# Top-32 attention with a gated feed-forward: batch 0 takes its score products in plain fp32 on 64 partitions

## The chip, the core and the metric

The kernel runs on one core of one Trainium2 chip. The metric is device time in microseconds (us) of one execution. The kernel before takes 1626.93 us, the median of 3 runs (1625.65 to 1627.8).

## What is computed

The inputs are q, k and v of 8 batches, 8 heads, 576 positions and 64 head dimensions, and three weights of a gated feed-forward network. Cut to what matters:

```
scores = 1/sqrt(64) * q @ k.T                   # (8, 8, 576, 576)
kth    = the 32nd largest score of each row
scores = where(scores >= kth, scores, -1e9)
attn   = exp(scores - rowmax) / sum             # softmax over the kept ones
x      = (attn @ v), heads side by side         # (4608, 512)
out    = (sigmoid(x @ w_gate) * (x @ w_val)) @ w_out
```

The second part has 1536 hidden units, and 4608 tokens in all.

## The kernel before

Three dimensions cut the attention. A batch has four head pairs (p), and each head has five query tiles (i): four of 128 rows, and a last one in which the remaining 64 rows of both heads of a pair stand side by side. One step of the program is one (pair, query tile): 20 steps to a batch, 16 with two heads one after the other (J = 2) and 4 with the shared tile (J = 1). The steps of a batch run in two groups; in batch 0 the first group holds query tiles 0 to 2 of all four pairs (12 steps), the second tiles 3 and 4 (8 steps).

A step goes through these stages:

- `load_keys`, `load_queries` (L154, L172) bring transposed keys and queries into memory. The host has written each of them twice, on partitions 0 to 63 and again on 64 to 127. The keys of a head (128x576) are rounded by ScalarE (ACT) to the short format fp32r (L161), and on partitions 64 to 127 GpSimd (POOL) puts the rest, raw minus rounded, in their place, in two halves (L163). A query tile (128x256) is rounded on ACT (L176) to `qh`, and POOL makes `ql`, raw minus rounded (L177). A product over 128 partitions with `qh` and one with `ql` then add up to the product of the unsplit numbers, to the precision of the parts.
- `scores` (L180) makes these two fp32r products for each half of 288 keys (L195), and ACT copies a head's row of 576 from PSUM (L202). The PSUM tile has one buffer.
- `select` (L243) is mostly VectorE (DVE): maxima of 8 segments (L260), three rounds of maxima and replacement over the 64 candidates (L264, L266); then ACT's sign (L272), POOL's product with it (L278), a last maximum on DVE (L286), ACT's exponential (L209) and DVE's masked product (L214).
- `turn` and `weigh` (L289, L308): TensorE (PE) transposes the probabilities (L297, L302), multiplies them by the values in plain fp32 (L316 to L324), and the result is stored as a rounded part and a rest, `xh` and `xl`.
- `ffn` works on units of 384 tokens with fp32r weights and three products for each (L372 to L374, L391 to L393).

Before use, each of 18 weight blocks is split into two fp32r parts as well (`split_weight`, L116): two halves to a block, each with three DVE instructions (L136 to L138), three PE products (L144 to L146), and work of ACT and POOL (L135, L139, L141, L143, L147). Twelve blocks are split during the first group of batch 0, one to a step; the last six when the first unit of the feed-forward comes to them.

What orders the work: the main loop (L437) issues scores two steps ahead (`AHEAD`), queries four (`ASK`) and the keys and values of the next pair (`fetch`); the feed-forward is let in by the number of tokens done (L462), with a lag of `BEHIND` = 480 tokens. A scheduler then lays the recorded instructions out on each engine by its own model of their times; each engine takes its list in order.

Of the kernel before, what the change touches and what calls it, by code (L numbers as in the profile page):

```python
# [28 lines left out]
def tile_topk_attention_then_gated_ffn(  # L29
# [32 lines left out]
    BEHIND = 480  # L62

    LOADED, HELD = 12, 0

    const = ctx.enter_context(tc.tile_pool(name="const", bufs=1))
    bi = ctx.enter_context(tc.tile_pool(name="bi", bufs=4))
# [86 lines left out]
    def load_keys(b, p, nm):  # L154

        ks = []
        for h in (2 * p, 2 * p + 1):
            raw = bkr.tile([P, S], F32, tag="kraw", name=f"kraw_{nm}_{h}")
            nc.sync.dma_start(raw, k[b, h])
            kt = bk.tile([P, S], F32R, tag="k", name=f"k_{nm}_{h}")  # L160
            nc.scalar.activation(kt, raw, AF.Copy)  # L161
            for c in (slice(0, HALF), slice(HALF, S)):
                nc.gpsimd.tensor_tensor(kt[D:, c], raw[D:, c], kt[D:, c], op=ALU.subtract)  # L163
            ks.append(kt)
        return ks
# [4 lines left out]
        return vt  # L170

    def load_queries(b, i, p):  # L172
        raw = bqr.tile([P, 2 * P], F32, tag="qraw", name=f"qraw_{b}_{i}_{p}")
        nc.sync.dma_start(raw, q[b, i, p])
        qh, ql = [bq.tile([P, 2 * P], F32R, tag=t, name=f"{t}_{b}_{i}_{p}") for t in ("qh", "ql")]
        nc.scalar.activation(qh, raw, AF.Copy)  # L176
        nc.gpsimd.tensor_tensor(ql, raw, qh, op=ALU.subtract)  # L177
        return qh, ql

    def scores(qs, ks, i, nm):  # L180

        J = 2 if i < NT else 1
        s = bs.tile([P, 2, S], F32, tag="s", name=f"s_{nm}")
        for j in range(J):
            ps = ps_s.tile([P, 2, 512], F32, tag="s", name=f"pss_{nm}_{j}")
            for half in range(2):

                parts = [(j, 0, HALF, half * HALF)]
                if i == NT:

                    m = S - REM - HALF
                    parts += [(1, 0, HALF, REM)] if half == 0 else [(1, 0, m, REM + HALF), (1, m, REM, 0)]
                todo = [(x, part) for part in parts for x in qs]
                for t, (x, (h, o, n, k0)) in enumerate(todo):
                    nc.tensor.matmul(  # L195
                        ps[:, half, o : o + n],
                        x[:, h * P : (h + 1) * P],
                        ks[h][:, k0 : k0 + n],
                        start=t == 0,
                        stop=t == len(todo) - 1,  # L200
                    )
# [371 lines left out]
```

## Time and profile before

| | |
|---|---|
| median of 3 runs | 1626.93 us |
| the profiled execution's own time | 1628.2 us |
| its span, first to last instruction | 1626.3 us |
| mean granted TensorE clock | 0.977 |
| PE busy | 1546.3 us (95%), 10226 instructions |
| PE weight loads busy | 1399.8 us (86%) |
| DVE busy | 1285.6 us (79%) |
| POOL busy | 1238.9 us (76%) |
| ACT busy | 1174.1 us (72%) |

The shares are means over a start, a long middle and an end, which differ; the stretches are read apart in the rows further down. A granted clock of 1.00 is TensorE's upper level, 2.4 GHz, and 0.50 the lower, 1.2 GHz; a mean in between says how long each level was held. Matmul ends are modelled, so what a matmul costs in a row of them is read from the distance between starts. A plain fp32 matmul leaves two records in the trace, an fp32r matmul one.

### The profile page before, as it was taken

The numbers are of one execution on the slowest core, as the hardware profiler recorded it, in microseconds if no ns is written. First come the engines' busy times: TensorE is split into PE (matmuls) and PEld (weight loads), VectorE is DVE, ScalarE is ACT, GpSimd is POOL, SyncE is SP. The second block draws the span as 40 slices with busy tenths as digits, with TensorE's granted clock in tenths as the row PEclk, the third lists the DMA queues.
The fourth block names the chain that finished last, engine by engine and source line by source line (L and its number), as shares of the span: only waits on it lengthen the run. The fifth ranks groups of instructions, "written<-read, shape, count | busy, mean of one in ns | idle before, by whom it ended". The sixth has DMA issues, their size and how long they took to land.

```text
span 1626.3 us, 33530 instructions
## 1 busy us (share of the span) xinstructions
PE 1546.3 (95%) x10226; PEld 1399.8 (86%) x10226; DVE 1285.6 (79%) x5748; ACT 1174.1 (72%) x2643; POOL 1238.9 (76%) x1959
## 2 busy tenths in 40 slices
PE   5777899899999999999999999999999999999998
PEld 3444797689999999989999999999899999999997
DVE  6999868988988778878888778889888778878310
ACT  8898668877777777677777777778677777767321
POOL 8889868898876887787776896788876987776413
PEclk8887999999999999999999999999999999999999
DMA  7546754566565665566564665565555665554574
GB/s 259 186 161 201 266 203 167 186 225 217 189 218 178 219 236 198 184 207 227 193 206 178 219 239 195 196 230 195 203 199 178 216 224 198 184 198 164 195 265 178
DMA packets 89182, 332.58 MB, mean 204 GB/s; under 512 B 9888, under 2 KB 36512, under 8 KB 62112
## 3 DMA queue, kind: packets, MB, share of 16 engines
q1 hardware_dynamic: 88992, 330.34, 58.7%
q8 instruction: 83, 1.36, 0.3%
q14 instruction: 107, 0.88, 0.2%
HBM read 301.99 MB, written 28.31 MB: 203 GB/s over the span
## 4 chain that ended last, share of the span: by engine, by line
PE 75%; DVE 5%; POOL 5%; ACT 4%; issue 1%; POOLq 0%; ACTq 0%; DVEq 0%
PE pz L372 11%; PE pz L374 11%; PE pz L373 11%; PE pss L195 8%; PE po L316 6%; PE pt L297 6%; PE po L391 6%; PE po L392 5%; PE po L393 5%; PE po L318 2%; POOL u L278 2%; DVE e L214 2%; ACT e L209 1%; PE po L327 1%; DVE kths L286 1%
## 5 line engine op out<-in xcount | busy, mean ns | idle before, releaser
L278 POOL TENSOR_TENSOR u<-s,under 128x288 f32<-128x288 f32 x576 | 446.1, 796 | 89.0 <-ACT under L272 82.7
L260 DVE MAX8 cand<-s 128x8 f32<-128x72 f32 x2304 | 346.7, 217 | 81.4 <-ACT s L202 80.7
L372 PE MATMUL pz<-xh,w 128*128 128x384 f32 x1120 | 383.3, 344 | 1.7 <-ACT part L398 1.7
L373 PE MATMUL pz<-xl,w 128*128 128x384 f32 x1120 | 379.5, 339 | 0.0
L374 PE MATMUL pz<-xh,w 128*128 128x384 f32 x1120 | 379.4, 339 | 0.0
L214 DVE SCALAR_TENSOR_TENSOR e<-s,kths,e 128x576 f32<-128x576 f32 x288 | 297.1, 1035 | 1.9 <-ACT e L209 1.8
L286 DVE MAX8 kths<-u 128x8 f32<-128x584 f32 x288 | 219.7, 763 | 71.0 <-POOL u L279 69.0
L272 ACT ACTIVATE under<-s,leads 128x576 bf16<-128x576 f32 x288 | 223.2, 776 | 42.2 <-DVE leads L264 38.0
L209 ACT ACTIVATE e<-s,st 128x576 f32<-128x576 f32 x288 | 210.7, 773 | 57.5 <-POOL st L268 57.4
L380 POOL TENSOR_TENSOR gl<-gf,gh 128x384 fp32r<-128x384 f32 x144 | 153.5, 1066 | 88.8 <-ACT gh L379 86.3
L202 ACT ACTIVATE s<-pss 128x576 f32<-128x576 f32 x288 | 185.3, 643 | 39.0 <-PE pss L195 38.9
L372 PEld LDWEIGHTS pz<-xh,w 128*128 128x128 f32 x1120 | 210.9, 188 | 2.5 <-ACT part L398 2.0
L195 PE MATMUL pss<-k,qh 128*128 128x288 f32 (+2 forms) x672 | 200.6, 316 | 13.1 <-ACT qh L176 6.6
L373 PEld LDWEIGHTS pz<-xl,w 128*128 128x128 f32 x1120 | 210.9, 188 | 0.4 <-issue 0.3
L374 PEld LDWEIGHTS pz<-xh,w 128*128 128x128 f32 x1120 | 210.7, 188 | 0.0
L298 ACT ACTIVATE et<-pt 128x384 f32<-128x384 f32 x384 | 180.8, 489 | 36.5 <-PE pt L297 35.6
L297 PE MATMUL pt<-ident,e 128*128 128x128 f32 x1152 | 188.0, 280 | 16.6 <-DVE e L214 14.9
L392 PE MATMUL po<-gl,w 128*128 128x384 f32 x560 | 192.2, 344 | 0.4 <-POOL gl L380 0.4
L391 PE MATMUL po<-gh,w 128*128 128x384 f32 x560 | 189.4, 352 | 1.8 <-ACT part L398 0.9
L393 PE MATMUL po<-gh,w 128*128 128x384 f32 x560 | 189.7, 340 | 0.0
L195 PE MATMUL pss<-k,ql 128*128 128x288 f32 (+2 forms) x672 | 185.1, 298 | 1.0 <-POOL ql L177 1.0
L297 PEld LDWEIGHTS pt<-ident,e 128*128 128x128 f32 x1152 | 145.4, 144 | 37.9 <-DVE e L214 16.2
(100 smaller groups left out, 3339.2 us busy)
## 6 DMA issues: line engine op xcount, KB each, us to landing
w<-ws SPq DMA_DIRECT2D x210, 1024.0 KB, 5.0
v<-in_v_dram SPq DMA_DIRECT2D x64, 352.0 KB, 3.4
qraw<-in_q_dram SPq DMA_DIRECT2D x160, 128.0 KB, 2.8
kraw<-in_k_dram SPq DMA_DIRECT2D x64, 288.0 KB, 3.4
wraw<-in_w_dram SPq DMA_DIRECT2D x36, 512.0 KB, 4.1
ws<-wsplit SPq DMA_DIRECT2D x36, 512.0 KB, 4.0
out_dram<-acc SPq DMA_DIRECT2D x48, 192.0 KB, 3.6
```

Of the source, the lines that this page charges most:

```text
L195: nc.tensor.matmul(ps[:, half, o : o + n], x[:, h * P : (h + 1) * P], ks[h][:, k0 : k0 + n], start=t == 0, stop=t == len(todo) - 1,)
L214: nc.vector.scalar_tensor_tensor(e[:, j], s[:, j], kth[j], e[:, j], op0=ALU.is_ge, op1=ALU.mult, accum_out=st[:, 4 + j : 5 + j])
L260: nc.vector.max(cand[:, j, 8 * g : 8 * g + 8], s[:, j, g * SEG : (g + 1) * SEG])
L278: nc.gpsimd.tensor_tensor(u[:, j, c], s[:, j, c], under[:, j, c], op=ALU.mult)
L286: nc.vector.max(kths[:, at[j] : at[j] + 8], u[:, j])
L297: nc.tensor.transpose(pt[:, c], ef[:, k0 : k0 + P], ident)
L372: nc.tensor.matmul(ps, wt[:, u, 0, d], xh, start=d == 0, stop=False)
L373: nc.tensor.matmul(ps, wt[:, u, 0, d], xl, start=False, stop=False)
L374: nc.tensor.matmul(ps, wt[:, u, 1, d], xh, start=False, stop=d == NP - 1)
L391: nc.tensor.matmul(ps, wt[:, e % 2, 0, f], gh, start=f == 0, stop=False)
L392: nc.tensor.matmul(ps, wt[:, e % 2, 0, f], gl, start=False, stop=False)
L393: nc.tensor.matmul(ps, wt[:, e % 2, 1, f], gh, start=False, stop=f == FG - 1)
```

## The change

Batch 0 no longer splits keys and queries. Its keys and queries are loaded as fp32, the first 64 partitions only, and one plain fp32 product over 64 partitions stands in place of the two fp32r products over 128. The other seven batches are as before.

```diff
+    WHOLE = 1
...
     def load_keys(b, p, nm):
         ks = []
         for h in (2 * p, 2 * p + 1):
+            if b < WHOLE:
+                kt = bk.tile([P, S], F32, tag="k", name=f"k_{nm}_{h}")
+                nc.sync.dma_start(kt[:D], k[b, h][:D])
+                ks.append(kt)
+                continue
...
     def load_queries(b, i, p):
+        if b < WHOLE:
+            whole = bq.tile([P, 2 * P], F32, tag="qh", name=f"q_{b}_{i}_{p}")
+            nc.sync.dma_start(whole[:D], q[b, i, p][:D])
+            return (whole,)
...
     def scores(qs, ks, i, nm):
         J = 2 if i < NT else 1
+        K = D if len(qs) == 1 else P
...
                     nc.tensor.matmul(
                         ps[:, half, o : o + n],
-                        x[:, h * P : (h + 1) * P],
-                        ks[h][:, k0 : k0 + n],
+                        x[:K, h * P : (h + 1) * P],
+                        ks[h][:K, k0 : k0 + n],
```

In instructions: 8 roundings of keys and 20 of queries leave ACT; 16 key differences and 20 query differences leave POOL; 168 fp32r products leave PE and 84 plain fp32 ones come (64 of 288 columns, and four times 288, 288, 288, 224 and 64). The DMAs of batch 0's keys and queries keep their number, 8 and 20, at half the bytes.

The scheduler lays out all lists anew. Lines of the changed kernel stand 2 further down in `split_weight`, and 12 further down from `scores` on (L214 is then the eviction of the scores, L226 the masked product, L272 and L276 the maxima, L298 the last maximum, L384 the first feed-forward product).

ACT at the start of the program, before: five roundings (L161, L176) stand ahead of the first score eviction (`s`, L202).

```order
L161 ACTIVATE k_0_0_165<-kraw_0_0_163 128x576
L161 ACTIVATE k_0_1_171<-kraw_0_1_169 128x576
L176 ACTIVATE qh_0_0_179<-qraw_0_0_177 128x256
L176 ACTIVATE qh_1_0_185<-qraw_1_0_183 128x256
L176 ACTIVATE qh_2_0_191<-qraw_2_0_189 128x256
L135 ACTIVATE wt_lead_0_230<-wraw_0_228 128x512
L139 ACTIVATE wsplit_227<-wraw_0_228 128x512
L202 ACTIVATE s_0_0_201<-pss_0_0_0_202 128x576
```

The same place in the changed kernel:

```order
L214 ACTIVATE s_0_0_177<-pss_0_0_0_178 128x576
L137 ACTIVATE wt_lead_0_198<-wraw_0_196 128x512
L141 ACTIVATE wsplit_195<-wraw_0_196 128x512
L137 ACTIVATE wt_lead_1_215<-wraw_1_213 128x512
L141 ACTIVATE wsplit_195<-wraw_1_213 128x512
L214 ACTIVATE s_0_0_177<-pss_0_0_1_182 128x576
```

The first eviction of scores now stands ahead of the first weight block's work, and the five roundings are gone.

PE where the first feed-forward product comes (`pz`), before; `wrest` is the first product of the last half of the twelfth weight block, and `pss` are scores of the last head pair:

```order
L297 MATMUL pt_3_1_1_2387<-ident,e_3_1_2009 128x128 x2
L195 MATMUL pss_3_3_0_2285<-k_3_6_1154,qh_3_3_1988 128x288
L195 MATMUL pss_3_3_0_2285<-k_3_6_1154,ql_3_3_1989 128x288
L195 MATMUL pss_3_3_0_2285<-k_3_6_1154,qh_3_3_1988 128x288
L195 MATMUL pss_3_3_0_2285<-k_3_6_1154,ql_3_3_1989 128x288
L144 MATMUL wrest_1_1691<-wraw_1_1688,ident 128x512
L372 MATMUL pz_0_0_0_2146<-xh_0_684,w_0_2142 128x384
```

The same place in the changed kernel:

```order
L339 MATMUL po_3_0_1894<-ident,inv_3_0_1779 128x128
L317 MATMUL pt_4_0_1_2067<-ident,e_4_0_1751 64x128
L309 MATMUL pt_3_1_0_2191<-ident,e_3_1_1831 128x128 x3
L146 MATMUL wrest_1_1547<-wraw_1_1544,ident 128x512
L384 MATMUL pz_0_0_0_1959<-xh_0_612,w_0_1955 128x384
```

In both, the feed-forward stands right behind that `wrest`, which needs DVE's work on the block's last half (`wraw`). Ahead of it stand 154 of batch 0's 168 score products before, and 75 of 84 now; 123 transposes (L297) before and 120 now. On DVE, the list up to that `wraw` is 19 instructions shorter now: ten segment maxima, four candidate maxima, three replacements, one masked product and one product of `weigh` come later. Up to the `wraw` of the last of the 18 blocks it is 16 shorter.

## Rows read from the trace of the kernel before

**Rows 1.** Busy time of each engine in four stretches of the span (start, length, then busy us and number of instructions of each engine, the mean granted TensorE clock, the DMA share and rate).

```profile
0.00:180.00 180.00, 123.99 (x573) 79.05 (x573) 164.51 (x672) 156.90 (x327) 157.74 (x240) 0.83 0.62 208
180.00:260.00 80.00, 77.84 (x529) 72.54 (x527) 60.64 (x257) 50.25 (x115) 60.53 (x97) 1.00 0.59 209
260.00:330.00 70.00, 62.45 (x349) 48.33 (x347) 64.14 (x256) 62.17 (x133) 56.61 (x81) 0.95 0.59 195
330.00:1560.00 1230.00, 1223.33 (x8446) 1142.22 (x8447) 991.35 (x4556) 890.84 (x2042) 947.04 (x1526) 1.00 0.59 204
```

The columns of busy time are PE, PE's weight loads, DVE, ACT, POOL.

**Rows 2.** DVE's waits in the first 180 us (who waited for whom: us in total, times, the longest).

```profile
DVE wt_lead L136 <- ACT wt_lead L135: 9.6, 1, 9.6
DVE kths L286 <- POOL u L279: 2.8, 4, 1.4
```

**Rows 3.** The timeline, in order of time, around the places where the feed-forward begins (start, us, engine, line, operation, tiles, count, idle before and its releaser), and the line of the `wrest` products over the whole run (min, median and max in ns; first and last start).

```profile
179.29 1.17 PE L144 MATMUL wrest<-wraw,ident 128*128 128x512 f32 x2 [0.90 <-DVE wraw L137]
179.87 0.76 PE L372 MATMUL pz<-xh,w 128*128 128x384 f32 x1
...
L144 PE MATMUL wrest<-wraw,ident x72: 609/617/1224, 10.8 to 324.4; 128*128 128x512 f32 x72
```

**Rows 4.** The timeline of the first 12 us, some rows of it.

```profile
3.51 1.38 ACT L161 ACTIVATE k<-kraw 128x576 fp32r<-128x576 f32 x2 [0.98 <-DMA kraw<-in_k_dram]
...
6.07 1.30 ACT L176 ACTIVATE qh<-qraw 128x256 fp32r<-128x256 f32 x3 [1.17 <-DMA qraw<-in_q_dram]
...
8.91 0.67 ACT L135 ACTIVATE wt_lead<-wraw 128x512 f32<-128x512 f32 x1 [1.55 <-DMA wraw<-in_w_dram]
...
9.61 0.43 DVE L136 TENSOR_SCALAR wt_lead<-wt_lead 128x512 uint32<-128x512 uint32 x1 [9.61 <-ACT wt_lead L135]
...
10.04 0.64 ACT L202 ACTIVATE s<-pss 128x576 f32<-128x576 f32 x1
...
11.14 1.03 DVE L260 MAX8 cand<-s 128x8 f32<-128x72 f32 x7
```

**Rows 5.** What the change takes away: groups of equal instructions in the first 240 us (ACT) and the first 180 us (POOL), with count, busy us, mean ns. The counts hold some of batch 1's too.

```profile
L176 ACT ACTIVATE qh<-qraw 128x256 fp32r<-128x256 f32 x27 | 11.1, 417 | 2.1 <-DMA qraw<-in_q_dram 1.2 <-PE pss L195 0.5
L161 ACT ACTIVATE k<-kraw 128x576 fp32r<-128x576 f32 x16 | 10.8, 677 | 2.8 <-DMA kraw<-in_k_dram 2.3 <-PE pss L195 0.3
...
L163 POOL TENSOR_TENSOR k<-kraw,k 64x288 fp32r<-64x288 f32 x26 | 23.8, 941 | 4.0 <-ACT k L161 3.3
L177 POOL TENSOR_TENSOR ql<-qraw,qh 128x256 fp32r<-128x256 f32 x21 | 17.3, 827 | 0.9
```

**Rows 6.** DVE's groups in the first 165 us (count, busy us, mean ns).

```profile
L214 DVE SCALAR_TENSOR_TENSOR e<-s,kths,e 128x576 f32<-128x576 f32 x27 | 29.4, 1089 | 0.0
...
L137 DVE SCALAR_TENSOR_TENSOR wraw<-wraw,wt_lead 128x512 uint32<-128x512 uint32 x22 | 19.9, 906 | 0.1
L136 DVE TENSOR_SCALAR wt_lead<-wt_lead 128x512 uint32<-128x512 uint32 x23 | 14.6, 633 | 9.6 <-ACT wt_lead L135 9.6
L138 DVE TENSOR_SCALAR wt_lead<-wraw 128x512 uint32<-128x512 uint32 x22 | 13.9, 633 | 0.1
```

**Rows 7.** The same lines and the segment maxima over the whole run (count: min, median and max in ns), a query difference on POOL, and one row of the timeline with eight segment maxima.

```profile
L214 DVE SCALAR_TENSOR_TENSOR e<-s,kths,e x288: 791/950/1601, 28.0 to 1512.4; 128x576 f32<-128x576 f32 x144
L137 DVE SCALAR_TENSOR_TENSOR wraw<-wraw,wt_lead x36: 667/996/1432, 10.1 to 320.6; 128x512 uint32<-128x512 uint32 x36
L136 DVE TENSOR_SCALAR wt_lead<-wt_lead x36: 400/472/1023, 9.6 to 318.6; 128x512 uint32<-128x512 uint32 x36
L138 DVE TENSOR_SCALAR wt_lead<-wraw x36: 400/510/1080, 10.8 to 323.7; 128x512 uint32<-128x512 uint32 x36
L260 DVE MAX8 cand<-s x2304: 204/217/239, 11.1 to 1504.6; 128x8 f32<-128x72 f32 x192
...
L177 POOL TENSOR_TENSOR ql<-qraw,qh x160: 720/738/1352, 7.5 to 1474.8; 128x256 fp32r<-128x256 f32 x160
...
24.39 1.16 DVE L260 MAX8 cand<-s 128x8 f32<-128x72 f32 x8
```

**Rows 8.** PE's timeline at the upper clock level: two fp32r score products one after the other, then plain fp32 products of 256 columns with 64 weight columns (L316, two records each, side by side with L317's on the other 64 columns of the array), then one with 128 weight columns (L318) and what follows it.

```profile
406.58 0.29 PE L195 MATMUL pss<-k,qh 128*128 128x288 f32 x1
406.72 0.29 PE L195 MATMUL pss<-k,ql 128*128 128x288 f32 x1
...
411.06 0.38 PE L316 MATMUL po<-et,v 128*64 128x256 f32 x1
...
411.28 0.38 PE L316 MATMUL po<-et,v 128*64 128x256 f32 x1
...
56.01 0.70 PE L318 MATMUL po<-et,v 128*128 128x256 f32 x2
56.55 0.38 PE L327 MATMUL po<-ident,inv 128*128 128x128 f32 x2
```

**Rows 9.** PE's two largest waits in the first 180 us (us in total, times, the longest).

```profile
PE wrest L144 <- DVE wraw L137: 17.2, 16, 2.8
PE pt L297 <- DVE e L214: 14.4, 14, 2.7
```

**Rows 10.** PE's timeline at the lower clock level: two fp32r score products one after the other.

```profile
13.17 0.45 PE L195 MATMUL pss<-k,qh 128*128 128x288 f32 x1
...
13.41 0.45 PE L195 MATMUL pss<-k,ql 128*128 128x288 f32 x1
```

## The prediction, on record before the run

> **What bounds the kernel now.** First the busy times by stretch [rows 1]. From 330 to 1560 us PE is busy 1223 of 1230 us at a clock of 1.00: it is the bound there, and whatever comes 1 us sooner or later into this stretch ends as much sooner or later. The first 180 us, in which the change acts, are different: PE is busy 124 us, at a mean clock of 0.83 (so about a third of the time at the lower level), and DVE 164.5 us. DVE's waits there [rows 2] come to 9.6 us ahead of its first instruction and 2.8 us later on; it never waits for scores. So DVE bounds this stage. The stage ends when the feed-forward begins: its first product starts at 179.87 us, behind a `wrest` product that had waited for DVE [rows 3]. From 180 to 260 us PE is full (77.8 of 80), from 260 to 330 us nobody is (PE 62.5, DVE 64.1 of 70), until the last weight block is split at 324.4 us [rows 1, 3].
>
> The question is therefore what the change does to DVE's stage, to which it gives no instruction and from which it takes none, and what it adds to PE behind that stage.
>
> **The change part by part.** The sum is made against the profiled execution, 1628.2 us (span 1626.3 us), which lies 1.3 us above the median of 1626.93 us; I carry the differences over to the median.
>
> *The start.* Before, keys are there at 3.51 us and the first query at 6.07 us; roundings on ACT and differences on POOL follow, DVE's first work is a weight block at 9.61 us, and the first segment maximum starts at 11.14 us [rows 4]. Now the scores need the query alone, at 6.07 us. Two plain fp32 products (0.5 us each at the upper clock, 1 us at the lower, see below) and the eviction (0.64 us [rows 4]) let DVE begin at 7.7 to 8.7 us, in place of 9.61. I take **-1 us**; the ends are 0 (DVE only swaps scores and weights) and -2 us. The order shows the eviction first on ACT, so it is not queued behind the weight block.
>
> *ACT.* 8 roundings of 0.677 us and 20 of 0.417 us leave [rows 5]: 13.8 us. DVE did not wait for ACT after its start [rows 2], so they count as nothing: DVE's own list covers them.
>
> *POOL.* 16 x 0.941 and 20 x 0.827 us leave [rows 5]: 31.6 us, a fifth of POOL's 157.7 busy us in the stage [rows 1]. DVE waits for POOL's results only 2.8 us there [rows 2]. But DVE's instructions themselves are drawn out. L214 takes 791 ns at its shortest and 1089 ns in the mean of this stage, L137 667 and 906, L136 and L138 400 and 633 [rows 6, 7], while the segment maxima stay between 204 and 239 ns over the whole run [rows 7]. The excess is 27 x 0.298 + 22 x 0.239 + 23 x 0.233 + 22 x 0.233 = 23.8 us. The maxima show that it is no general slowness; POOL, busy 88% of the stage, is what these four could collide with. If the excess falls with POOL's busy time, a fifth of it goes: **-5 us**. The ends: 0, if POOL's other work moves into the freed time and collides as often, and -13 us (second rival).
>
> *The order.* Up to the last half of the twelfth block DVE's list is now 19 instructions shorter. One is an L214 (1.09 us [rows 6]); the others I price like segment maxima, eight of which take 1.16 us in a row [rows 7], 0.145 each: 18 x 0.145 = 2.6. So the feed-forward is let in **-4 us** earlier. This work is not saved; it comes after 180 us, where DVE is busy 60.6 of 80 us and PE is full [rows 1]. Since DVE's list up to the last block is shorter too (by 16), I don't take it back in the mixed stretch. Ends: 0, where it is paid there after all, and -4.
>
> *PE.* Two fp32r products of 288 columns start 0.14 us apart [rows 8]: 0.28 us for the pair. Plain fp32 records of 256 columns start 0.22 us apart where the weights are 64 columns wide; a product is two, so 0.44, and 0.495 us for 288 columns. With 128 weight columns, as here, a product of 256 columns holds the next one back by 0.54 us (56.01 to 56.55 [rows 8]), that is 0.60 for 288. I take 0.55, since here two products with the same weights follow each other and half of the weight loading may hide. In units of 288 columns there are 80 of them: 80 x (0.55 - 0.28) = 21.6 us more on PE (17 to 26). The half depth is credited with nothing: no row here shows a product of this shape on 64 partitions; if it halved the cost, PE's work would be unchanged and the next term 0. 75 of the 84 products stand ahead of the feed-forward, in the stage where PE is idle 56 us [rows 1]: cost 0, covered by DVE's list (third rival if not). Behind it stand 9 products where there were 7 pairs, and 3 more transposes (0.11 us each): 9 x 0.55 - 7 x 0.28 + 0.3 = **+3 us**, all on the path. Ends 0 and +4.
>
> *DMA.* Half the bytes of 28 loads: nothing, the loads were ahead of their users. Batch 1's keys can now be fetched earlier, since batch 0 leaves the buffers for raw keys free; with a DMA share of 0.62 in this stage [rows 1] I cost that at nothing too. If a weight block is late for it, DVE's list stalls at its L136.
>
> Sum: -1 - 5 - 4 + 3 = -7 us. The profiled execution would take 1621.2 us, the median **1620 us**. The ends add up to 1626.93 - 2 - 13 - 4 + 0 = 1608 and 1626.93 + 4 = 1631.
>
> **The rivals.**
>
> *The relief is handed back (0.26).* POOL fills the freed time with its other work, DVE's four instructions collide as often, and what the order gained is paid between 260 and 330 us. Left are the start and PE's term: 1626.93 - 1 + 3 = 1629 us; with a third of the lock's relief 1627. For it: in the mixed stretch DVE, ACT and PE are all near 90% [rows 1], so that a head start can be lost. Against it: POOL's total work really falls, and DVE's list ahead of the end of that stretch is shorter.
>
> *Each difference that leaves frees a whole collision (0.14).* 36 POOL instructions of some 0.738 us [rows 7] go. If each had stopped one DVE instruction for the half of its length that is left on average, DVE gains 36 x 0.37 = 13 us in place of 5: 1612 us. For it: L214's maximum, 1601 ns, lies 0.8 us above its minimum, about one POOL instruction. Against it: 23.8 us of excess over the whole stage would have come for more than half from a fifth of POOL's work. The Trainium skill (SBUF, "Who interferes with whom") gives the rule for this: VectorE and GpSimd share a pair of ports as an exclusive lock, and the one that issues second "fully blocks". By that rule the unchanged maxima, with one input, would stay out of it, and the trace agrees (204 to 239 ns).
>
> *PE becomes the engine that DVE waits for (0.15).* At the lower clock level two fp32r products start 0.24 us apart [rows 10], a pair takes 0.48 us, and a plain product, at twice 0.495, 0.99. Should all 75 run there, PE gets 75 x 0.51 = 38 us more: 162 of 180 us. It takes its list in order, and waits 31.6 us for DVE, in `wrest` and transposes [rows 9]. It decides itself at 18 us: if more of these waits than that stay, scores come late, DVE waits for L202, and the stage grows. With 25 us left of them it grows by 7, and with the +3 behind it the kernel takes 1637 us. For it: PE's clock of 0.83. Against it: a busier PE comes later to those waits and finds them shorter, and scores are issued two steps ahead.
>
> That the change does not do what it says has no chance of its own: the order shows 84 plain products and no rounding of batch 0.
>
> **How the numbers follow.** The forecast has 0.45, the rivals 0.26, 0.14 and 0.15. A measurement of this kernel can tell about 0.2% from no change, 3.3 us: faster is below 1623.7, slower above 1630.2. The forecast and the second rival are faster (0.59), less 0.03 for a forecast with small terms: 0.56. The first rival is no change (0.26 and those 0.03: 0.29). The third is slower: 0.15. The range goes from 1610 to 1631: it holds the forecast, the first two rivals and the bounds but the farthest, and leaves out most of the third. The forecast's own range is 1614 to 1624.
>
> **What would show it.** Right: the first feed-forward product (L384) at about 170 us, the last `wrest` product at 313 to 318 us; DVE's L226, L138, L139 and L140 shorter in the first 165 us by 5 us in sum; PE busy some 20 us more in that stage, at no lower clock; DVE still without waits for L214. The start of the score products at about 6 us shows the first term. Wrong: those four DVE lines as long as before (first rival), a first feed-forward product before 165 us (second), or waits of L272 for L214 and PE above 150 of the stage's us (third). If plain products follow each other by far less or more than 0.55 us at the upper level, the PE term was mis-sized.

## The result and the profile after

The changed kernel takes 1636.81 us (1634.64 to 1638.98, 5 runs) beside 1627.17 us of the kernel before on the same chip: 1.006 times as long [1.0045, 1.0074]. It is slower by 9.6 us, where 7 us less were forecast. The profiled execution is the median itself, with a span of 1635.0 us. All medians below are of fast executions: one of run 2 (1891 us) and two of run 13 (3031 and 3853 us) were slow and are left out.

Busy time by stretch, in the columns of [rows 1] (PE, its weight loads, DVE, ACT, POOL, granted clock, DMA share and rate), and two stretches of 10 us inside the first; then the first of these two stretches in the kernel before:

```profile
0.00:180.00 180.00, 149.38 (x513) 81.37 (x514) 147.71 (x638) 137.21 (x278) 121.49 (x196) 0.79 0.56 183
180.00:260.00 80.00, 79.08 (x541) 72.06 (x540) 61.59 (x261) 54.40 (x126) 58.07 (x94) 1.00 0.60 207
260.00:330.00 70.00, 65.86 (x382) 51.14 (x381) 65.35 (x259) 64.54 (x141) 60.47 (x88) 1.00 0.66 228
...
30.00:40.00 10.00, 10.00 (x21) 5.16 (x19) 7.74 (x49) 7.56 (x14) 4.63 (x7) 0.50 0.22 83
...
50.00:60.00 10.00, 10.00 (x31) 5.68 (x32) 7.86 (x38) 6.74 (x12) 4.54 (x9) 0.50 0.27 99
```

```profile
30.00:40.00 10.00, 6.73 (x16) 3.67 (x15) 8.82 (x40) 9.05 (x20) 9.59 (x14) 0.50 0.78 254
```

PE does 25 us more in the first 180 us than before, DVE 17 us less: DVE is no longer the engine that is always at work. From 30 to 40 and from 50 to 60 us PE's records leave not a moment free, all of it at the lower level, 1.2 GHz, and in both DVE is idle for over 2 us, POOL for over 5, and the DMA share falls to 0.22 and 0.27. The lower level from 30 to 40 us is not new: the kernel before has it there too, with PE busy 6.73 of 10 us. What DVE, and then ACT, waited for in the first 180 us (us in total, times, the longest; [rows 2] are the same view of before):

```profile
DVE cand L272 <- ACT s L214: 12.3, 6, 9.0
DVE wt_lead L138 <- ACT wt_lead L137: 9.5, 7, 2.8
DVE xf L345 <- ACT rs L342: 7.6, 3, 4.2
DVE kths L298 <- POOL u L291: 1.8, 2, 1.4
```

```profile
ACT wt_lead L137 <- DMA wraw<-in_w_dram: 15.6, 11, 3.9
ACT s L214 <- PE pss L207: 12.1, 8, 5.8
ACT rs L342 <- PE po L339: 5.7, 2, 3.4
```

Apart from its start (9.0 us) DVE waits 3.3 us for scores, 9.5 us for weights and 7.6 us for a product of `weigh`. Before, it waited for weights once, at its start, and for `weigh` not at all [rows 2]. The wait for weights goes on to ACT, and from there to a transfer. Why the transfer was late stands in the waits of SP's queue over the same 180 us, after and then before:

```profile
SPq L150 <- ACT wsplit L149: 39.0, 16, 6.1
SPq L130 <- PE wrest L146: 23.2, 12, 6.5
SPq L182 <- PE pss L207: 22.1, 6, 5.1
...
SPq L182 <- PE pt L309: 9.8, 6, 3.2
```

```profile
SPq L174 <- POOL ql L177: 37.3, 19, 6.8
SPq L148 <- ACT wsplit L147: 29.9, 12, 5.4
SPq L128 <- DVE wt_lead L138: 23.3, 13, 3.8
SPq L159 <- POOL k L163: 22.3, 11, 4.0
SPq L128 <- PE wrest L144: 6.6, 7, 1.8
```

Before, the queue that loads everything, and stores the split weights, was held by POOL, ACT and DVE, and by PE's `wrest` for 6.6 us. Now PE holds it for 55 us in its three lines (before in all of its lines for 17), and ACT for 39 us at the stores. The sum of all its waits has not grown, 143 us before and 141 after; what has changed is whom it waits for: a weight half can be fetched when PE's `wrest` has read the half that lies in its buffer (there are two), a query of batch 0 when PE's plain products have read one that lies in its buffer (there are four). One turn of this loop in the timeline (start, us, engine, line, operation, idle before and its releaser):

```profile
34.11 2.29 PE L207 MATMUL pss<-k,q 64*128 64x288 f32 x4
...
36.33 2.07 PE L146 MATMUL wrest<-wraw,ident 128*128 128x512 f32 x2
...
38.48 2.40 SPq L130 DMA_DIRECT2D wraw<-in_w_dram  x2
38.62 1.84 PE L146 MATMUL wrest<-wraw,ident 128*128 128x512 f32 x2
...
42.35 0.66 ACT L137 ACTIVATE wt_lead<-wraw 128x512 f32<-128x512 f32 x1 [0.68 <-DMA wraw<-in_w_dram]
...
43.11 0.45 DVE L138 TENSOR_SCALAR wt_lead<-wt_lead 128x512 uint32<-128x512 uint32 x1 [1.82 <-ACT wt_lead L137]
```

Two plain products at the lower level stand in PE's list ahead of `wrest`; the transfer is issued as `wrest` ends (38.48 us), lands 3.9 us later, and ACT and DVE have waited for it. This is one turn; how much of the loss goes round this way the waits alone do not tell. What answers to [rows 3], [rows 4] and [rows 6] (the feed-forward's begin, the first scores, DVE's four lines in the first 165 us):

```profile
184.22 1.17 PE L146 MATMUL wrest<-wraw,ident 128*128 128x512 f32 x2 [0.92 <-DVE wraw L139]
...
184.80 0.76 PE L384 MATMUL pz<-xh,w 128*128 128x384 f32 x1
```

```profile
6.06 2.26 PE L207 MATMUL pss<-k,q 64*128 64x288 f32 x4 [6.06 <-DMA q<-in_q_dram]
...
8.35 0.65 ACT L214 ACTIVATE s<-pss 128x576 f32<-128x576 f32 x1 [5.83 <-PE pss L207]
9.03 1.18 DVE L272 MAX8 cand<-s 128x8 f32<-128x72 f32 x8 [9.03 <-ACT s L214]
...
10.35 0.66 ACT L137 ACTIVATE wt_lead<-wraw 128x512 f32<-128x512 f32 x1 [1.35 <-DMA wraw<-in_w_dram]
```

```profile
L226 DVE SCALAR_TENSOR_TENSOR e<-s,kths,e 128x576 f32<-128x576 f32 x26 | 25.6, 985 | 0.0
L139 DVE SCALAR_TENSOR_TENSOR wraw<-wraw,wt_lead 128x512 uint32<-128x512 uint32 x21 | 17.8, 845 | 0.0
L140 DVE TENSOR_SCALAR wt_lead<-wraw 128x512 uint32<-128x512 uint32 x21 | 10.9, 521 | 0.0
L138 DVE TENSOR_SCALAR wt_lead<-wt_lead 128x512 uint32<-128x512 uint32 x22 | 10.7, 486 | 9.5 <-ACT wt_lead L137 9.5
```

The feed-forward begins 4.9 us later than before, and from there to the end of the span it takes 1450.2 us where it took 1446.4. DVE's four lines did become shorter, and by more than forecast: 26 x 0.104 + 21 x 0.061 + 21 x 0.112 + 22 x 0.147 = 9.6 us. So DVE was relieved, and lost it in waits. Not all of it is POOL's doing, though: run 4 below shortens the same lines while POOL keeps its differences.

### The profile page after: what moved, and what is told of

The parts are those of the page before. It is cut to its first block, busy times and chain, and to the rows that moved or that the text cites. A ratio compares the mean times of both kernels' runs of the same rounds, so it can differ in the third digit from the quotient of the medians.

```text
span 1635.0 us, 33416 instructions
## 1 busy us (share of the span) xinstructions
PE 1584.1 (97%) x10226; PEld 1408.7 (86%) x10226; DVE 1281.5 (78%) x5748; ACT 1163.2 (71%) x2615; POOL 1208.8 (74%) x1923
## 4 chain that ended last, share of the span: by engine, by line
PE 70%; DVE 10%; POOL 6%; ACT 5%; issue 2%; DMA 2%; SPq 0%; POOLq 0%; DVEq 0%; ACTq 0%
PE pz L384 10%; PE pz L386 10%; PE pz L385 10%; PE pss L207 8%; PE po L328 5%; PE pt L309 5%; PE po L403 5%; PE po L404 5%; PE po L405 5%; DVE e L226 3%; POOL u L290 2%; DVE cand L272 2%; DVE kths L298 2%; PE po L330 2%; DMA wraw<-in_w_dram 1%
## 5 line engine op out<-in xcount | busy, mean ns | idle before, releaser
L272 DVE MAX8 cand<-s 128x8 f32<-128x72 f32 x2304 | 347.0, 217 | 105.9 <-ACT s L214 104.8
L384 PE MATMUL pz<-xh,w 128*128 128x384 f32 x1120 | 383.0, 343 | 0.0
L226 DVE SCALAR_TENSOR_TENSOR e<-s,kths,e 128x576 f32<-128x576 f32 x288 | 301.8, 1054 | 1.1 <-ACT e L221 0.9
L298 DVE MAX8 kths<-u 128x8 f32<-128x584 f32 x288 | 219.3, 761 | 54.0 <-POOL u L291 51.8
L214 ACT ACTIVATE s<-pss 128x576 f32<-128x576 f32 x288 | 185.4, 644 | 55.7 <-PE pss L207 55.3
L384 PEld LDWEIGHTS pz<-xh,w 128*128 128x128 f32 x1120 | 210.5, 188 | 0.8 <-issue 0.6
L207 PE MATMUL pss<-k,qh 128*128 128x288 f32 (+2 forms) x588 | 167.9, 303 | 4.2 <-ACT s L214 4.0
L207 PE MATMUL pss<-k,ql 128*128 128x288 f32 (+2 forms) x588 | 159.6, 294 | 0.0
```

Source lines behind the costliest of these rows:

```text
L207: nc.tensor.matmul(ps[:, half, o : o + n], x[:K, h * P : (h + 1) * P], ks[h][:K, k0 : k0 + n], start=t == 0, stop=t == len(todo) - 1,)
L226: nc.vector.scalar_tensor_tensor(e[:, j], s[:, j], kth[j], e[:, j], op0=ALU.is_ge, op1=ALU.mult, accum_out=st[:, 4 + j : 5 + j])
L272: nc.vector.max(cand[:, j, 8 * g : 8 * g + 8], s[:, j, g * SEG : (g + 1) * SEG])
L298: nc.vector.max(kths[:, at[j] : at[j] + 8], u[:, j])
L384: nc.tensor.matmul(ps, wt[:, u, 0, d], xh, start=d == 0, stop=False)
```

## The experiments

Sixteen kernels ran. Theory A at the start: the products' depth of 64 costs PE time and clock; the rivals stand in each expectation.

**1. The same products in two row groups.** Half 0 of the keys on partitions 0 to 63, half 1 on 64 to 127 (the host has both copies).

```diff
-                nc.sync.dma_start(kt[:D], k[b, h][:D])
+                nc.sync.dma_start(kt, k[b, h])
...
+                rows = slice(half * D, half * D + D) if len(qs) == 1 else slice(0, P)
...
-                        x[:K, h * P : (h + 1) * P],
-                        ks[h][:K, k0 : k0 + n],
+                        x[rows, h * P : (h + 1) * P],
+                        ks[h][rows, k0 : k0 + n],
```

> The change with its plain fp32 products of the two halves of a row on different partitions: half 0 on 0 to 63, half 1 on 64 to 127 (keys and queries loaded on all 128, as before the change). Count and shape of the products are the change's. Theory (PE's plain products make the scores and what is queued behind them late, and DVE waits): if two products on different halves of the rows run side by side, four records of a score tile take about half of the 2.29 us that they take at the lower clock in the changed kernel, PE's busy time in the first 180 us falls from 149 us to about 125, the first feed-forward product comes at 168 to 174 us in place of 184.8, and the time is 1617 to 1624 us. Rival 1 (they don't run side by side): as the change, 1635 to 1639 us. Rival 2 (PE's time is not what holds the stage; late weight blocks or the list's order are): the products run side by side, and the time still stays above 1630 us.

Measured: 1625.88 us, 0.9996 [0.9986, 1.0006]: between the range of the theory and that of rival 2, with PE's busy time at 129.6 us and the first feed-forward product at 177.4 us, over 3 us later than the theory had it.

**2. Plain products over all 128 partitions**, loads as in 1, the eviction's scale halved because each score then counts twice.

```diff
-        K = D if len(qs) == 1 else P
+        K, unit = P, 0.5 if len(qs) == 1 else 1.0
```

> The change on all 128 partitions: keys and queries are loaded twice, as before the change, and one plain fp32 product over 128 partitions gives twice the score, which the eviction halves. Count and columns of PE's products are the change's. Theory A (the low clock of 0.50 in 30 to 40 and 50 to 60 us, where PE is busy without a break, comes with products on half of the partitions): the clock in the first 180 us rises from 0.79 to 0.83 or more, and the time falls by 3 us or more, to 1634 us or less. Theory B (it comes with plain fp32 products as such): clock 0.77 to 0.81 and 1635 to 1639 us.

Measured: 1630.87 us, 1.0028 [1.0018, 1.0038]. PE's rows for two plain products of a head, with what follows them: on 128 partitions at the upper level, at the lower one, and at the upper one behind a pause of PE; then at the upper level in the changed kernel (its lower one, 2.29, stands above), then in row groups:

```profile
29.29 1.13 PE L207 MATMUL pss<-k,q 128*128 128x288 f32 x4
30.25 1.06 PE L146 MATMUL wrest<-wraw,ident 128*128 128x512 f32 x2
...
72.71 2.12 PE L207 MATMUL pss<-k,q 128*128 128x288 f32 x4
74.62 0.85 PE L309 MATMUL pt<-ident,e 128*128 128x128 f32 x3
...
94.83 1.24 PE L207 MATMUL pss<-k,q 128*128 128x288 f32 x4 [2.12 <-ACT s L214]
```

```profile
66.29 1.23 PE L207 MATMUL pss<-k,q 64*128 64x288 f32 x4
67.45 0.50 PE L148 MATMUL wrest<-wsplit,plus 128*128 128x512 f32 x1
```

```profile
169.63 0.76 PE L207 MATMUL pss<-k,q 64*128 64x288 f32 x4
```

Half the depth is not cheaper but dearer: from the start of two products to the start of what follows lie 1.16 us on 64 partitions (67.45 - 66.29) and 0.96 on 128 at the upper level, 2.22 (36.33 - 34.11, above) and 1.91 at the lower. The starts of the single records show where: inside the row they lie 0.24 us apart at either depth (0.48 at the lower level). On 64 partitions the second record starts 0.35 us (0.64) behind the first, and the next product, of full depth, 0.33 us (0.61) behind the last; on 128 partitions, with PE at work before, mostly 0.24 (0.48) there too, and 0.35 for the second record where PE had paused. Where another product on 64 partitions follows one on 64, it starts 0.24 us behind. In these rows, then, the price stands at the change between products of full and of half depth, and not in each product. Two row groups run side by side. In the first 180 us PE has 129.6 us of work in row groups and a clock of 0.86, and 137.2 us at 0.90 on 128 partitions, beside 149.4 at 0.79. Theory A holds as far as it goes, in the clock (0.90) and in the time (under 1634): 6 us lie between depth 64 and depth 128, 11 us between depth 64 and row groups.

**3. The relief alone:** the kernel before without batch 0's differences (rounded products; `qh` stands in for `ql`). **4. The plain products alone:** the changed products, but all roundings and differences still done into tiles that nobody reads.

```diff
-            for c in (slice(0, HALF), slice(HALF, S)):
+            for c in (slice(0, HALF), slice(HALF, S)) if b else ():
...
+        if b == 0:
+            qh = bq.tile([P, 2 * P], F32R, tag="qh", name=f"qh_{b}_{i}_{p}")
+            nc.scalar.activation(qh, raw, AF.Copy)
+            return qh, qh
```

> The kernel before with only POOL's relief: in batch 0 keys and queries are rounded by ACT as before, and the differences on POOL are left out; the two products use the rounded query twice (so what is left out is the rest of the split: scores are of rounded numbers, scaled back by 1/4). PE has the same products as before. Theory (the relief is worth something, and PE's plain products ate it): the four DVE lines of the forecast get shorter by 4 us or more in sum in the first 165 us, the first feed-forward product comes at 168 to 176 us in place of 179.9, the time is 1616 to 1623 us. Rival (POOL's relief is worth nothing to DVE's stage): 1625 to 1629 us.

> The change with only PE's part: batch 0's scores are plain fp32 products over 64 partitions, but ACT still rounds batch 0's keys and queries and POOL still takes the differences, which nobody uses; the DMAs are those of before. Theory (relief and PE's cost are two terms that add up): slower than the change by what the relief gives, 1642 to 1652 us. Rival (PE alone sets the stage's length, and the relief changes nothing there): 1635 to 1639 us, as the change.

Measured: the relief alone 1619.14 us, 0.9955 [0.9939, 0.9970], as the theory had it; the products alone 1635.81 us, 1.0059 [1.0044, 1.0075], as the rival had it. So the relief is worth 8.0 us where PE is as before, and nothing (-1.0 us) under the plain products. The two parts, -8.0 and +8.7, do not add up to +9.6. In run 4 the first 180 us, and DVE's four lines in the first 165 us, read:

```profile
0.00:180.00 180.00, 145.31 (x521) 79.53 (x522) 152.86 (x639) 147.74 (x303) 145.98 (x227) 0.84 0.59 198
```

```profile
L234 DVE SCALAR_TENSOR_TENSOR e<-s,kths,e 128x576 f32<-128x576 f32 x24 | 23.9, 998 | 0.0
L139 DVE SCALAR_TENSOR_TENSOR wraw<-wraw,wt_lead 128x512 uint32<-128x512 uint32 x23 | 19.8, 862 | 0.4 <-issue 0.3
L138 DVE TENSOR_SCALAR wt_lead<-wt_lead 128x512 uint32<-128x512 uint32 x23 | 14.3, 623 | 4.7 <-ACT wt_lead L137 4.7
L140 DVE TENSOR_SCALAR wt_lead<-wraw 128x512 uint32<-128x512 uint32 x22 | 11.8, 534 | 0.1
```

Although no difference leaves POOL in run 4, these lines are 5.6 us shorter than before [rows 6]; in run 3, where 36 leave and PE is as before, 7.0 us (means of 1025, 837, 584 and 522 ns). So part of the 9.6 us of the changed kernel comes without the relief; why was not taken apart. The clock of run 4 is no lower than before (0.84 beside 0.83), and the loss is there all the same.

**5 to 7. A third buffer for raw weight halves**, in the changed kernel, in the row groups (6) and in the kernel before (7). To make room, raw queries get two buffers and raw keys one.

```diff
-    ... (("signs", 1), ("raw", 2), ("parts", 2))}
+    ... (("signs", 1), ("raw", 3), ("parts", 2))}
```

> The changed kernel with three buffers for raw weight halves in place of two; to make room, raw queries have two buffers and raw keys one. Theory B: part of the loss goes through the raw weight buffers (PE's wrest products come late, the buffers are freed late, the next weight half is fetched late, ACT's L137 waits 15.6 us for it and DVE's L138 9.5 us for ACT). Then L137's waits for the transfer fall under 7 us, DVE's waits for L137 under 4 us, the first feed-forward product comes at 179 to 182 us in place of 184.8, and the kernel takes 1631 to 1634 us in place of 1636.8. Rival P: PE's own time sets the stage's length whatever is fetched; the waits only move from L138 to the maxima (L272 waiting for the eviction L214), the first feed-forward product stays at 183 to 186 us, and the kernel takes 1635 to 1638 us.

> The row-group version (half 0 of the keys on partitions 0 to 63, half 1 on 64 to 127; 1625.9 us) with three buffers for raw weight halves (raw queries two, raw keys one). Theory D: that version loses 5 to 7 us in its first 37 us because weight halves stand behind key and query loads in SP's queue and wait for one of two buffers; ACT waits 7.3 and 4.3 us for them. With a third buffer the third half is issued ahead of the keys of later pairs: DVE's waits for ACT's L137 fall from 4.3 to under 2 us, the first feed-forward product comes at 171 to 174 us in place of 177.4, and the kernel takes 1619 to 1623 us. Rival: the loss lies elsewhere (in the eviction that DVE waits for), and the time stays at 1625 to 1627 us.

> The kernel before with the same three raw weight buffers (raw queries two, raw keys one) and nothing else. Theory: there DVE waits only for its first weight half, and SP only 4 us for buffers, so a third buffer has nothing to give: 1625 to 1628 us, first feed-forward product at 178 to 181 us. Fewer raw key buffers could cost up to 2 us. Rival: the third buffer is worth some us by itself, in any kernel: 1618 to 1623 us; then what the versions with it gain says nothing about the change.

Measured: 1622.04 us, 0.9967 [0.9951, 0.9982]; row groups 1610.38 us, 0.9901 [0.9886, 0.9916]; before 1624.79 us, 0.9990 [0.9980, 0.9999]. The third buffer gives the changed kernel 14.8 us and the row groups 15.5, more than any expectation had, and the kernel before 2.2 (0.2 us under its theory's range). The waits of SP's queue for `wrest` in the first 180 us, in 5 and in 6:

```profile
SPq L130 <- PE wrest L146: 10.2, 9, 2.6
```

```profile
SPq L130 <- PE wrest L146: 2.3, 4, 0.8
```

They were 23.2 us in the changed kernel. But the gain does not go with these waits. In the row groups and on 128 partitions with two buffers (runs 1 and 2) they are no longer than in the kernel before (6.6):

```profile
SPq L130 <- PE wrest L146: 5.3, 6, 1.6
```

```profile
SPq L130 <- PE wrest L146: 2.7, 5, 1.2
```

and there the third buffer gives 15.5 us and, in run 16, 18.4. So with its smaller pools the third buffer is worth 15 to 18 us to each kernel that neither rounds nor splits batch 0, whether PE's `wrest` holds the queue or not. With the buffer the scheduler also lays the weights' work earlier (the first feed-forward product comes at 145 to 146 us in all three), so the expected start times of 171 to 182 us say nothing; the totals do. The row groups with three buffers beat both kernels, by 16.6 and 26.4 us.

**8. As 6, with batch 0's queries in the raw queries' buffers** (`bqr`, `qraw` in place of `bq`, `qh`).

> As the row-group version with three raw weight buffers, but batch 0's queries lie in the three buffers of the raw queries (so that those of batch 1 cannot be fetched ahead of them), raw keys have one buffer, and qh and ql three each. Theory D: with two queries of batch 1 fewer ahead of the early weight halves, and one query of batch 0 fewer ahead of the first, the first weight half lands 0.5 us sooner, and the kernel takes 1 to 3 us less than the version before it: 1617 to 1621 us. Rival: the order of these small loads is worth nothing (within 0.7 us of that version), or three buffers for qh and ql cost the later batches 1 to 4 us, which shows as a longer time from the first feed-forward product to the end than 1446 us.

Measured: 1615.76 us, 0.9943 [0.9929, 0.9956]: 5 us longer than 6, against the theory, and more than the 1 to 4 us of the rival. DVE starts with a weight half in place of scores there, at 10.2 us; the rest of the loss was not traced.

**9, 10. The controls to 5 and 6:** the smaller pools, but two weight buffers.

> The control to the changed kernel with three raw weight buffers (1622.0 us): the changed kernel with raw queries cut to two buffers and raw keys to one, but the weights still with two. Theory B (the raw weight buffers carry 15 us of loss): the cut gives nothing, 1634 to 1639 us, and ACT's L137 goes on waiting over 10 us for the transfer in the first 180 us. Rival O (what helped was that batch 1's raw keys and queries can no longer be fetched ahead of the weight halves): 1622 to 1630 us.

> The same control to the row-group version with three raw weight buffers (1610.4 us): the row-group version with raw queries cut to two buffers and raw keys to one, weights with two. Theory B: 1624 to 1628 us as without the cut (1625.9). Rival O: 1611 to 1620 us.

Measured: 1631.79 us, 1.0022 [1.0008, 1.0036], and 1627.83 us, 1.0002 [0.9993, 1.0012]. The first lies between the two ranges (ACT's L137 waits 8.7 us for the transfer, under theory B's 10), the second in theory B's. Smaller pools alone move the time by -5.0 and +1.9 us, so of 14.8 us the buffer itself has 9.8 in the changed kernel, and in row groups 17.4. A few us either way come with any new layout of the lists.

**11, 12. Relief alone (3) and products alone (4) with three weight buffers.**

> The kernel before with batch 0's differences left out on POOL (rounded products, qh used twice: the scores of batch 0 are only rounded ones) and three raw weight buffers. With two buffers this relief alone gave 7.9 us. Theory A (parts add up: relief, product cost, raw buffers): the row-group version, which has the same relief and about the same PE time, won 14.4 us over the kernel before with three buffers (1624.8), so this one takes 1608 to 1613 us. Rival R (the relief stays what it was with two buffers): 1615.5 to 1618.5 us; then the row-group version won 6 us by something else, the keys and queries that need no rounding before the first scores above all.

> The changed kernel's plain products on 64 partitions with the roundings and differences of batch 0 still done (their results unused; with two raw weight buffers 1635.8 us), and three raw weight buffers. Theory A: the half-depth products cost the same 11 us as between the changed kernel and the row-group version with three buffers (1622.0 and 1610.4), so 1624.8 + 11: 1633 to 1639 us. Rival: with three buffers PE's late wrest products no longer hold up the weights, and the plain products cost only what lies behind the stage, some 3 us: 1625 to 1630 us.

Measured: 1612.86 us, 0.9905 [0.9889, 0.9922], and 1630.09 us, 1.0022 [1.0009, 1.0036]. The first is as theory A had it, the second lies at the edge of the rival's range and 3 us under theory A's.

**13 to 15. Loads held back.** Is it PE that holds the weights up, or do batch 0's keys, which no raw buffer throttles now, stand ahead of them in SP's queue? Later key loads of batch 0 and all raw loads of batch 1 wait for a score tile, through a tiny POOL write into their target: up to 34 of them.

```diff
+                if after is not None:
+                    nc.gpsimd.tensor_scalar(kt[:, 0:1], after[:, 0, 0:1], 1e-9, None, op0=ALU.add)
...
-                fetch(n + FETCH)
-                ask(n + ASK)
+                fetch(n + FETCH, staged.get(n))
+                ask(n + ASK, staged.get(n))
```

> The changed kernel (1636.8 us), with two raw weight buffers as it has them, but with every later key load of batch 0 and every raw key and query load of batch 1 held back until a score tile of the step that asks for it is there (one tiny POOL write from that tile into the load's target). So no key or query is fetched far ahead of the weight halves, as the roundings' buffers saw to in the kernel before. Theory D (the loads that run ahead in SP's queue delay the weight halves): ACT's L137 waits under 6 us for the transfer in the first 180 us in place of 15.6, and the kernel takes 1624 to 1631 us. Rival B (the weight halves are late because PE's late wrest products hold the two buffers): the waits stay above 10 us and the kernel takes 1633 to 1638 us.

> The row-group version (1625.9 us) with the same loads held back, two raw weight buffers. Theory D: its loss in the first 37 us goes, 1616 to 1621 us. Rival B: two buffers limit it however the loads stand, 1624 to 1628 us.

> The row-group version with three raw weight buffers (1610.4 us) with the same loads held back. Theory D: the fourth and fifth weight halves, which still stood behind ten key and query loads, come sooner: 1605 to 1609 us. Rival: three buffers already cover that order, 1609 to 1613 us, or the held keys come late and DVE waits for scores, over 1613 us.

Measured: the changed kernel 1633.55 us, 1.0031 [1.0020, 1.0041]; row groups 1630.83 us, 1.0020 [1.0010, 1.0030]; row groups with three buffers 1618.37 us, 0.9941 [0.9927, 0.9956]. In the first, ACT still waits 13.8 us for weight transfers, as rival B had it, and the first 180 us read:

```profile
0.00:180.00 180.00, 147.82 (x590) 86.42 (x591) 155.98 (x678) 141.81 (x291) 122.78 (x206) 0.91 0.59 194
```

The clock is back at 0.91 and the time is not. The row groups lose 5 and 8 us by the holding: the first was in neither theory, the second was a case of the rival, but DVE waits only 0.6 us for scores there after its start. The POOL writes, which wait for scores in POOL's list, may be the reason, and that was not taken apart. As the holding has a cost of its own, run 13 alone does not clear the clock; with run 4 (0.84, and 8.7 us lost) the lower mean clock is not what the loss needs.

**16. Products over 128 partitions (2) with three weight buffers.**

> The plain products over all 128 partitions (scale halved; with two raw weight buffers 1630.9 us) with three raw weight buffers. Theory A: between the changed kernel (1622.0) and the row groups (1610.4) with three buffers lies PE's price; at 0.49 us in place of 0.59 for a product at the upper clock and a higher share of that clock, 4 to 8 of the 11.6 us go: 1614 to 1618 us. Rival: with three buffers PE's price no longer depends on the depth: 1620 to 1624 us.

Measured: 1612.44 us, 0.9899 [0.9881, 0.9917]: 9.6 us less than the changed kernel with three buffers, and 1.6 us under theory A's range. Beside the relief alone with three buffers (1612.9) products over 128 partitions cost nothing, those over 64 cost 9.2 us: with three buffers the whole price of the plain products is their half depth.

All medians in one table, in us:

| | two raw weight buffers | three |
|---|---|---|
| kernel before | 1627.2 | 1624.8 |
| relief alone (3, 11) | 1619.1 | 1612.9 |
| products of 64 partitions alone (4, 12) | 1635.8 | 1630.1 |
| both: the change (5) | 1636.8 | 1622.0 |
| relief, 128 partitions (2, 16) | 1630.9 | 1612.4 |
| relief, two row groups (1, 6) | 1625.9 | 1610.4 |

## Why the prediction was wrong

**The step that failed** is the one that costs 75 of the 84 plain products at nothing, "covered by DVE's list", together with the remark of the DMA term that a late weight block would stall DVE, which was given no price. The runs showed in its place: the products alone cost 8.7 us where +3 was forecast (run 4), and DVE, which had waited for none of the three, waits 20.4 us after its start: 9.5 for weights, 7.6 for a product of `weigh` and 3.3 for scores. What covers a longer PE is not DVE's list alone: PE's list and DVE's feed each other within one step through the scores, and through SP's queue. I had seen half of it ("If a weight block is late for it, DVE's list stalls at its L136"), but asked only whether there is bandwidth, not who frees the buffer that the transfer waits for. PE was idle for 56 of 180 us, but not at the times at which a transfer or DVE hangs on it, as the turn of the loop above shows for one of them. That batch 1's keys are fetched early was not shown to matter: held back (run 13), they leave 13.8 of ACT's 15.6 us. In the waits of SP's queue `wrest` stood in the profile of before, with 6.6 us: a view that I did not read.

**Term by term.** *Start*, -1: DVE begins at 9.03 in place of 9.61 us, so -0.6; but with four queries ahead of it the first weight half lands 1.4 us later (ACT's L137 at 10.35 in place of 8.91 us), which the sum did not have. *ACT*, 0: no run contradicts it. *POOL*, -5: the four lines gave 9.6 us in the changed kernel, but 5.6 of this also come where POOL is not relieved (run 4). *Order*, -4: together with POOL's term -9, and the relief alone, in a layout of its own, measured -8.0. As a sum these two were right as long as PE stays as it was; the split between them was not measured. *PE behind the feed-forward's begin*, +3: 1450.2 in place of 1446.4 us, +3.8, in this layout; in run 4 the first feed-forward product starts at 175.9 us and the rest takes 1457.6, so the place of that product does not part the loss cleanly. The forecast price of a product was close at the upper level (two in 1.16 us; forecast 1.10) and too low at the lower one (two in 2.22; forecast 1.98). *PE and DMA ahead of it*, 0: here is the miss. The stage was to end 10 us sooner and ended 4.9 us later.

**By the runs**, the way from the forecast's -7 to +9.6: 2 us for start, POOL and order (-10 in the sum; -8.0 for the relief alone, which has no earlier start), 5.7 for the products alone (+8.7 in place of +3), and 8.9 that neither part shows by itself with two raw weight buffers. With three, -11.9 and +5.3 stand against a measured -2.8, so 3.8 us remain. Runs 3 and 4 have no control with smaller pools, and these alone moved other kernels by -5.0 and +1.9, so the 5 us between the two remainders are no more than a new layout can do.

**The third rival** had the sign and, at 1637 us, the size. Its mechanism was half right. PE did become the engine that the stage waits for, at 149 busy us where 162 were reckoned; but the wait that it named, DVE for the scores' eviction, is 3.3 us after the start. With the 7.6 us for `weigh`, whose product PE delivers late, up to 10.9 of the 20.4 us come from PE by a direct way; the other 9.5 went round by the raw buffer, SP's queue, ACT and L138, which the rival did not name. Its point of decision, 18 of PE's 31.6 us of waits [rows 9], was not the right question: of these two waits 11.4 us are left (10.1 for L139, 1.3 for L226), less than 18, and the stage still grew. The first rival (relief handed back) falls with DVE's shortened lines, the second with run 3: 8 us, not 13.

**What stays open.** With two buffers the row groups take 6.7 us longer than the relief alone, although PE has about as much to do (129.6 and 125.4 us in the first 180). A third buffer takes this away, held loads do not, and smaller pools do not. Whether it is the order of the loads or the buffers' turn was not settled, since the holding had a cost of its own. What the plain products cost, and that half depth has a large part in it, is shown (runs 2, 3, 4 and 16). How much of it goes through the loop of `wrest` and the raw buffers is read from the waits and not shown, since kernels without long waits for `wrest` gain as much from the third buffer. The scheduler's earlier weights alone are not its gain: the kernel before gets them too (first feed-forward product at 145.6 us) and gains 2.2 us.

## What to carry to other kernels

An engine's idle time need not cover more work when others, or the buffers of a load, wait for its results. Before costing work at nothing, ask who waits for that engine and when, look at who frees the buffers that the load queue waits for, and read the queue's own waits by releaser. Its waits alone prove nothing, though: here their sum in the first 180 us is 143 us in run 3 and 141 in the changed kernel, and these lie 18 us apart. When a change takes work from one engine and gives work to another, ask what the first engine's waiting did for the order of the loads. Products of half depth between products of full depth were the dearest kind here; in row groups or over the full depth the same change, with one buffer more, gave 1.0% (0.8 to 0.9% beside the kernel before with that buffer).

## What the runs showed of the hardware

Plain fp32 products over 64 partitions, standing between products over 128, took longer than products over 128: 1.16 against 0.96 us from the start of two to the start of what follows at the upper level, 2.22 against 1.91 at the lower. Among themselves they followed each other at the same 0.24 us for a record (0.48); the difference lies at the change of depth. The Trainium skill (TensorE: Matmul & The Clock Gate, "LDWEIGHTS (loading the stationary operand)") has the time of a weight load depend on its columns and not on its depth; the traces agree, with 187 ns in the median for the loads of these products on 64 partitions and 190 ns on 128 (run 2).

Two such products on the two halves of the partitions took 0.76 us together, against 1.23 one after the other: row groups work for plain fp32.

The granted clock stood at 0.50 through two stretches in which PE was busy 10.00 us of 10; in the stretches of 10 us ahead of them it was busy 6.94 and 7.65 us at 0.66 and 0.67. In the kernel before it stood at 0.50 from 30 to 40 us too, with PE busy 6.73 us. In the first 180 us the mean clock was 0.79 with products on 64 partitions, 0.90 with products on 128 and 0.86 in row groups. That was not depth alone, since on 64 partitions it was 0.84 with the roundings kept (run 4) and 0.91 with held loads (run 13).
